# A chunked delta-rule recurrence with a gated MLP behind it: four kinds of small matmuls put into one run, both merges and the keys' products into another, and a first merge that fills all rows

## The chip, the core and the metric

The kernel runs on one core of one Trainium2 chip. The time is device microseconds of one execution. The kernel before takes 634.97 us (median of three executions, 634.14 to 635.45). The execution that was profiled took 633.96 us, of which 631.8 us are the span from the first to the last instruction.

## The reference

Attention by the delta rule, for 4 batches and 8 heads, 768 tokens, head size 48, and then a two-layer MLP with SiLU over all 3072 tokens:

```python
for t in range(S):
    kt, vt, bt = (k_n[:, :, t], v[:, :, t], beta[:, :, t, None])
    y[:, :, t] = np.einsum('bhd,bhde->bhe', q[:, :, t], state)
    v_old = np.einsum('bhde,bhd->bhe', state, kt)
    state = state + bt[:, :, :, None] * np.einsum('bhd,bhe->bhde', kt, vt - v_old)
x = y.transpose(0, 2, 1, 3).reshape(B * S, H * D)          # 3072 x 384
h = x @ w_in                                               # 384 x 2048
out = (h * (1.0 / (1.0 + np.exp(-h)))) @ w_out             # 2048 x 384
```

`k_n` is `k` divided by its norm. Everything is float32.

## The kernel before

The 768 tokens are cut into six chunks (`c` = 0 to 5) of 128, each of two halves of 64 (`hf` = 0, 1). Batches go in two groups (`g` = 0, 1) of two, so that one group has 16 heads; one group's work on one half is 16 matmuls of each kind, each with 48 or 64 rows and columns, and the two groups stand on opposite halves of the 128 rows. For a chunk from 1 on, the recurrence has these steps (`solve`, L1004):

- the triangular system of each head is inverted in blocks of 32, by VectorE, and the blocks of 32 are joined by two rows of products on TensorE, the first and the second merge (`merge`, L793; tile names `py` and `px`, matmuls on L808). The first merge's result is copied to `y`, the second's to `xi`;
- `keys` (L850, matmuls on L854): the state times the keys, added to the values `vf` by VectorE;
- `inner` (L861, L866): the inverse times `vf`, copied by ScalarE to `z`;
- `old` (L928, L932): the queries times the state, into a PSUM bank `pyc`. For the group with `hf != g`, ScalarE then reads a few words of the bank (tile `read`), since `new` adds to the same bank from other rows;
- `update` (L879, L886): keys times `z`, added to the state by VectorE, which the next `keys` and `old` need;
- `new` (L940, L945): scores times `z`, added to the bank of `old`; ScalarE copies the result out (`part`, `xT`).

Beside this stands the MLP of the chunk before: `hidden` (L1081, matmuls on L1088, 128 x 256), and `combine` (L1185, on L1200, 128 x 192), or for chunk 0 `project` (L1120, on L1132). The matmuls of the MLP use the full array of 128 x 128; those of the recurrence use tiles of it, 64 x 64, 64 x 48 or 32 x 32, four at a time.

Each float32 matmul is two passes, and each pass is a weight load and a matmul for the engine, so one matmul of the program is four TensorE instructions (a transpose is two). The trace counts passes.

The order on TensorE is written out by hand. A script of letters (`chunks`, L1656) calls the generators in turn: `s` is one step of the recurrence (`solve`), `r` one step of the MLP (three matmuls of 256 or four of 192), `i` a step of the inversion, `y`, `m`, `k`, `v` preparation and loads. `pin` (L78) binds each engine's instructions into the order in which they are called. So a change of the script moves instructions on all engines at once. In the kernel before, `solve` yields between almost all of the steps above, and the script puts `r` between them: a run of small matmuls, then 4 to 32 big ones, and so on.

## Time and profile before

| What | Value |
|---|---|
| Median of three executions | 634.97 us |
| Profiled execution | 633.96 us |
| its span | 631.8 us |
| TensorE matmuls, weight loads | 9390 passes each, busy 617.7 us and 543.3 us |
| VectorE, ScalarE, GpSimd busy | 415.5, 226.7, 94.0 us |
| Granted TensorE clock, mean | 0.989 |
| DMA queue q8, kind "instruction" | 74 packets, 1.21 MB |

The chain of work that ended last is followed back from the last instruction; a row of it is a start, a length and what ran or was waited for ("issue" is time in which the engine waited for nothing that the profile shows). A timeline row is the start, the length, the engine, line and operation; a matmul's end is modelled, so the distance between the starts says how long something held the engine. A view by windows has the busy time and, in brackets, the count of each engine's instructions. The strips of the DMA view cut a window into 40 equal slices; a digit is the share of the sixteen DMA engines that was busy in it.

### The profile page before, as it was taken

The page shows a single profiled execution, that of the slowest core. Times are in us where ns is not written, and L with a number is a line of the kernel's source. Part 1 is how long each engine was busy: PE and PEld are TensorE (multiplying, and loading weights), DVE is VectorE, ACT ScalarE, POOL GpSimd, SP SyncE. Part 2 cuts the span into 40 slices and gives each one's busy share as a digit, 9 for nine tenths or more (in the row PEclk, how much of TensorE's full clock was granted, in tenths as well). Part 3 has the DMA queues.
Part 4 walks back from the last instruction along what each step waited for, and adds up shares of the span by engine and source line. Part 5 has one row for each costly group of instructions (what it writes and reads, how often), then busy time and mean ns, then how long its engine had stood idle before and what let it go on. Part 6 is the DMA issues. An engine that isn't in the chain of part 4 may idle for free.

```text
span 631.8 us, 21374 instructions
## 1 busy us (share of the span) xinstructions
PE 617.7 (98%) x9390; PEld 543.3 (86%) x9390; DVE 415.5 (66%) x927; ACT 226.7 (36%) x516; POOL 94.0 (15%) x101
## 2 busy tenths in 40 slices
PE   8889989999999999999999999999999999999997
PEld 5578778666799989989989989989989989988997
DVE  6886779999667974546975554976444983345432
ACT  4657873332441122451122451122452122454210
POOL 5234631335020020020020010020002000000000
PEclk9869999999999999999999999999999999999999
DMA  9656506350459360459141359433254024010011
GB/s 175 134 141 199 170 16 149 116 86 4 101 100 186 62 108 4 95 107 188 34 92 20 72 125 156 65 75 44 52 113 95 2 75 62 17 38 1 0 26 26
DMA packets 136941, 52.61 MB, mean 83 GB/s; under 512 B 108672, under 2 KB 130432, under 8 KB 136848
## 3 DMA queue, kind: packets, MB, share of 16 engines
q1 hardware_dynamic: 136512, 51.09, 39.6%
q8 instruction: 74, 1.21, 0.9%
q10 hardware_dynamic: 336, 0.15, 0.1%
q14 instruction: 19, 0.16, 0.1%
HBM read 39.09 MB, written 9.96 MB: 78 GB/s over the span
## 4 chain that ended last, share of the span: by engine, by line
PE 93%; SPq 2%; DMA 1%; issue 1%; ACT 1%; DVE 0%
PE phid L1088 34%; PE px L1200 17%; PE py L1200 13%; PE po L1132 5%; PE pb_c L866 3%; PE pa L539 2%; SPq L144 2%; PE pb_c L1303 2%; PE pb_c L854 2%; PE pyc L945 2%; PE pc L1303 2%; PE pb_c L1132 2%; PE pb_c L886 2%; PE pa L1303 1%; PE pyc L932 1%; PE px L808 1%
## 5 line engine op out<-in xcount | busy, mean ns | idle before, releaser
L1088 PE MATMUL phid<-xT,w_in 128*128 128x256 f32 x960 | 214.9, 382 | 1.9 <-issue 1.7
L1088 PEld LDWEIGHTS phid<-xT,w_in 128*128 128x128 f32 x960 | 180.2, 190 | 26.9 <-issue 2.8
L1098 ACT ACTIVATE gT<-phid 128x512 f32<-128x512 f32 x72 | 42.9, 597 | 115.2 <-PE phid L1088 106.2
L656 DVE SCALAR_TENSOR_TENSOR rank<-g,step,x 128x31 f32<-128x31 f32 (+15 forms) x124 | 49.8, 402 | 23.3 <-DMA g<-blocks 19.8
L1200 PE MATMUL px<-sums_of_w,sums_of_g 128*128 128x192 f32 x320 | 56.6, 329 | 0.0
L1200 PE MATMUL py<-w_out,sums_of_g 128*128 128x192 f32 x320 | 56.2, 328 | 0.0
L1200 PEld LDWEIGHTS px<-sums_of_w,sums_of_g 128*128 128x128 f32 x320 | 52.2, 190 | 0.4
L1200 PEld LDWEIGHTS py<-w_out,sums_of_g 128*128 128x128 f32 x320 | 52.3, 190 | 0.3
L661 DVE TENSOR_TENSOR x<-x,rank 128x31 f32<-128x31 f32 (+15 forms) x124 | 42.5, 342 | 4.3
L477 POOL TENSOR_TENSOR vf<-vf,n_slot 128x768 f32<-128x768 f32 x10 | 14.8, 1492 | 175.4 <-DMA vf<-in_v_dram 129.9
L1183 DVE TENSOR_TENSOR sums_of_g<-gT 128x384 f32<-128x384 f32 (+1 forms) x48 | 24.6, 540 | 14.6 <-ACT gT L1098 14.5
L498 DVE STREAM_TRANSPOSE kq<-stage 128x512 f32<-128x512 f32 x28 | 28.4, 1121 | 6.8 <-DMA stage<-in_q_dram 3.5
L554 ACT COPY xT<-pyc 48x128 f32<-48x128 f32 (+2 forms) x120 | 31.1, 259 | 1.6
L1211 DVE TENSOR_TENSOR o<-o,kept 128x192 f32<-128x192 f32 (+1 forms) x29 | 11.5, 425 | 26.7 <-ACT kept L1208 26.7
L560 POOL COPY g<-x 64x256 f32<-64x256 f32 x4 | 5.0, 1244 | 150.8 <-DVE x L664 150.8
L891 DVE TENSOR_TENSOR state<-state,pb_c 128x384 f32<-128x384 f32 x22 | 11.2, 550 | 24.6 <-PE pb_c L886 24.6
L866 PEld LDWEIGHTS pb_c<-vf,xi 64*64 64x64 f32 x736 | 23.3, 138 | 3.2 <-issue 2.3
L866 PE MATMUL pb_c<-vf,xi 64*64 64x48 f32 x736 | 24.9, 223 | 0.1
L1132 PE MATMUL po<-w_out,gT 128*128 128x384 f32 x64 | 23.7, 491 | 0.0
L1200 PE MATMUL py<-w_out,gT 128*128 128x192 f32 x128 | 23.4, 331 | 0.0
L859 DVE TENSOR_TENSOR vf<-vf,pb_c 128x384 f32<-128x384 f32 x22 | 11.2, 550 | 18.3 <-PE pb_c L854 15.5
L1200 PE MATMUL px<-w_out,gT 128*128 128x192 f32 x128 | 22.4, 327 | 0.0
(293 smaller groups left out, 1094.5 us busy)
## 6 DMA issues: line engine op xcount, KB each, us to landing
vf<-in_v_dram SPq DMA_DIRECT2D x48, 96.0 KB, 2.8
out_dram<-o SPq DMA_DIRECT2D x42, 96.0 KB, 2.2
w_out<-in_moe_w_in_dram SPq DMA_DIRECT2D x4, 768.0 KB, 5.0
sums_of_w<-in_moe_w_out_dram SPq DMA_DIRECT2D x4, 768.0 KB, 4.6
kb<-in_k_dram SPq DMA_DIRECT2D x12, 192.0 KB, 4.5
kb<-in_k_dram SPq DMA_DIRECT2D x24, 96.0 KB, 4.0
raw<-in_moe_w_in_dram SPq DMA_DIRECT2D x3, 768.0 KB, 6.8
blocks<-ap SPq DMA_DIRECT2D x32, 64.0 KB, 1.9
```

Source lines behind the costliest of these rows:

```text
L477: pin(nc.gpsimd.tensor_tensor(out=vf, in0=vf, in1=of, op=ALU.mult))
L498: pin(nc.vector.transpose(out=kqs[c, b][:, :, j, :].rearrange("p a (i m) -> p a m i", i=T), in_=src.rearrange("p a (m d) -> p a m d", d=D) ...
L554: return pin(nc.scalar.copy(to, of))
L656: pin(nc.vector.scalar_tensor_tensor(out=tv, in0=g[:, 0:m, m : m + 1].to_broadcast([P, m, n]), scalar=step[:, m : m + 1], in1=x[:, m : m + ...
L661: yield pin(nc.vector.tensor_tensor(out=x[:, 0:m, m:T], in0=x[:, 0:m, m:T], in1=tv, op=ALU.add))
L866: yield pin(nc.tensor.matmul(pz[rows, n * D : (n + 1) * D], lhsT=xis[g][rows, u * H + 2 * p + e, :], rhs=vfs[c][rows, hf, g * HB + u, p, : ...
L1088: pin(nc.tensor.matmul(ph[:, j * GT : (j + 1) * GT], lhsT=w_in[:, a, (2 * f + j) * P : (2 * f + j + 1) * P], rhs=xTs[c, hf][:, a, :], star ...
L1098: pin(nc.scalar.activation(out=hidden_of(c, hf, f), in_=ph[:], func=ACTF.Silu, scale=-0.5 if in_blocks(c) else 0.5))
L1132: pin(nc.tensor.matmul(pos[i][:, 0:DM], lhsT=hidden_of(0, hf, f // 2)[:, at : at + C], rhs=w_outs[f // HFF][:, f % HFF, :], start=(f == 0) ...
L1183: pin(nc.vector.tensor_tensor(out=sums_of_g[:, k, fs], in0=of[0], in1=of[1], op=op))
L1200: pin(nc.tensor.matmul(to, lhsT=at, rhs=quarter(f, *b) if isinstance(b, tuple) else sums_of_w[b][:, f], start=start and f == 0, stop=f == ...
L1303: pin(nc.tensor.matmul(to[:, i * GT : (i + 1) * GT], lhsT=left(a, slice(f, f + 1))[:, 0], rhs=right(b), start=start and i == 0 and n == 0, ...
```

## The change

Four things change.

1. `made` now issues `inner` and `old` of both groups itself, group `1 - hf` first, and directly behind them `update` and `new`, one group after the other, with the two kinds alternating. Before, `update` of both groups alternated, then `new` of both, and the script stood between `old` and `update`. In the second half of chunk 5 (where nothing needs the state any more) the script still stands before `new`.
2. `merge` as the first merge multiplies by all 64 columns of the weights, so that its products fill all 64 rows of each half; the rows that nobody reads are copied too. One copy of 128 x 512 for each group replaces two of 32 x 512.
3. The script calls three steps together where a chunk begins (`s3`): first merge, `keys`, second merge. This holds for chunks 2 to 5.
4. The counts of `r` around the steps, and the end of the script of chunk 0, are adapted.

```diff
@@ merge
-                    left = aps[c, g][0][even, n // H, n % H, T:W]
-                    to, right = odd, xes[c][even, g * HH + n, :]
+                    left = aps[c, g][0][even, n // H, n % H, :]
+                    to, right = HALVES[k ^ g], xes[c][even, g * HH + n, :]
...
-            for rows in (slice(T, W), slice(W + T, P)):
-                (by_act, by_dve)[g](y[rows, g], of[rows])
+            (by_act, by_dve)[g](y[:, g], of)
@@ update
-        if c == NCH - 1 and hf == 1:
-            return
@@ new
-        copies.append(even_heads(c, g, hf, py))
+        copies.append((g, even_heads(c, g, hf, py)))
+        copies.sort(key=lambda of: of[0])
@@ made
-        together(update(c, 0, hf), update(c, 1, hf))
-        together(new(c, 0, hf), new(c, 1, hf))
-        for copy in copies:
+        gs = (1 - hf, hf)
+        for g in gs:
+            together(inner(c, g, hf), old(c, g, hf))
+        if (c, hf) == (1, 1):
+            follow(c)
+        if (c, hf) == (LAST, 1):
+            yield
+            together(new(c, 0, hf), new(c, 1, hf))
+        else:
+            for g in gs:
+                together(update(c, g, hf), new(c, g, hf))
+        for _, copy in copies:
             next(copy)
@@ solve
-            for g in range(2):
-                together(inner(c, g, hf), old(c, g, hf))
-            if hf == 1:
-                if c == 1:
-                    follow(c)
-            yield
-            made(c, hf)
+            yield from made(c, hf)
@@ chunks
-        5: "r s r2 s r s r2 s r s r s r s r2 s r s r2 s",
+        5: "r2 s3 r2 s r s r s r2 s r s r2 s r3",
```

How the order on TensorE changes where `inner` and `old` of chunk 3's second half end (`pb_c<-vf,xi` is `inner`, `pyc<-kq,state` is `old`, `pb_c<-z,kb` is `update`, `pyc<-ap,z` is `new`). Before:

```order
2349 L866 MATMUL pb_c_74<-vf,xi 64x48
2350 L932 MATMUL pyc<-kq,state_91 64x64
2351 L1200 MATMUL py<-w_out_110,sums_of_g 128x192 x4
2352 L1088 MATMUL phid<-xT,w_in 128x256 x3
2353 L886 MATMUL pb_c_75<-z,kb_77 48x48
2354 L886 MATMUL pb_c_73<-z,kb_77 48x48
```

and after the change:

```order
2350 L865 MATMUL pb_c_74<-vf,xi 64x48
2351 L929 MATMUL pyc<-kq,state_91 64x64
2352 L883 MATMUL pb_c_75<-z,kb_77 48x48
2353 L942 MATMUL pyc<-ap_3805,z 64x64
2354 L883 MATMUL pb_c_75<-z,kb_77 48x48
```

The seven big matmuls between have moved away, `update` follows `old` directly, and alternates with `new` of the same group instead of with `update` of the other.

The same for the end of chunk 3's first merge (`py<-xe,ap`), with `keys` behind it (`pb_c<-state,kq`). Before:

```order
2018 L808 MATMUL py<-xe,ap_3808 32x32
2019 L808 MATMUL py<-xe,ap_3856 32x32
2020 L1200 MATMUL px<-w_out_110,gT 128x192 x4
2021 L1200 MATMUL px<-sums_of_w,gT 128x192 x8
2022 L1200 MATMUL py<-w_out_109,sums_of_g 128x192 x4
2023 L854 MATMUL pb_c_74<-state_90,kq 64x48
```

and after the change:

```order
2024 L808 MATMUL py<-xe,ap_3804 64x32
2025 L808 MATMUL py<-xe,ap_3852 64x32
2026 L853 MATMUL pb_c_74<-state_90,kq 64x48
2027 L853 MATMUL pb_c_75<-state_91,kq 64x48
2028 L853 MATMUL pb_c_74<-state_90,kq 64x48
```

The sixteen big matmuls between have gone, and a product of the first merge is 64 rows high instead of 32; the second merge now follows behind `keys` as it did in this chunk before.

On ScalarE, around chunk 3's merges (`y<-py` and `xi<-px` are the merges' copies, `o<-px` and `o<-py` the MLP's). Before:

```order
227 L1098 ACTIVATE gT<-phid 128x512 x8
228 L554 COPY y<-py 32x512 x2
229 L1227 ACTIVATE o<-px 128x2x192
230 L554 COPY xi<-px 32x16x32 x2
231 L1230 ACTIVATE o<-py 128x192
232 L554 COPY z<-pb_c_73 128x2x4x48
233 L554 COPY z<-pb_c_74 128x2x4x48
234 L554 COPY read<-pyc 128x8
```

and after the change:

```order
228 L1231 ACTIVATE o<-py 128x192
229 L554 COPY y<-py 128x512
230 L554 COPY xi<-px 32x16x32 x2
231 L1234 ACTIVATE o<-px 128x192
232 L554 COPY z<-pb_c_73 128x2x4x48
233 L554 COPY read<-pyc 128x8
234 L554 COPY z<-pb_c_74 128x2x4x48
```

One copy of `y` is left of two, and the read of the bank, which now belongs to the group that comes first, stands between the two copies of `z`.

## The prediction

> **What bounds the kernel now.** First the page: the busy shares, then the shares of the chain that ended last.

> ```profile
> span 631.8 us, 21374 instructions
> ...
> PE 617.7 (98%) x9390; PEld 543.3 (86%) x9390; DVE 415.5 (66%) x927; ACT 226.7 (36%) x516; POOL 94.0 (15%) x101
> ...
> q8 instruction: 74, 1.21, 0.9%
> ...
> PE 93%; SPq 2%; DMA 1%; issue 1%; ACT 1%; DVE 0%
> ```

> TensorE is the bound: 98% busy, 93% of the chain, and nearly nothing waited for. So a gain can only come from the time that TensorE itself takes for its instructions or loses between them. Third, the chain around chunk 4's recurrence, since the change does the same there as in its neighbours.

> ```profile
> 425.53 2.60 PE px L1200 x16
> 428.13 1.22 PE py L808 x82
> 429.35 1.08 PE pb_c L854 x64
> 430.42 2.80 PE px L1200 x16
> ...
> 443.36 0.86 PE pb_c L886 x64
> 444.22 0.36 PE pyc L945 x23
> 444.59 0.23 issue
> 444.82 0.85 PE pyc L945 x41
> 445.67 1.50 PE py L1200 x8
> ...
> 453.64 0.18 PE pb_c L866
> 453.97 0.04 PE pb_c L866 x2
> ...
> 459.75 0.86 PE pb_c L886 x64
> 460.61 0.95 PE pyc L945 x64
> ```

> Three things are to be seen. Sixteen big passes take 2.60 us behind big ones and 2.80 us behind small ones: 0.20 us for a switch. A small run is dense in instructions: `update` and `new` are 128 passes, so 256 instructions with the weight loads, in 0.86 + 0.95 = 1.81 us, or 141 per us; sixteen big passes are 32 instructions in 2.60 us, 12 per us. And inside one `new` stands an "issue" of 0.23 us that waits for nothing: this run lasts 445.67 − 443.36 = 2.31 us, 0.50 more than the 1.81 of its twin at 459.75. Two like it stand elsewhere:

> ```profile
> 252.56 0.42 PE L886 MATMUL pb_c<-z,kb 64*48 64x48 f32 x18 [0.21 <-issue]
> 534.54 0.21 PE L808 MATMUL px<-xi,y 32*32 32x32 f32 x1 [0.24 <-issue]
> ```

> **What the stops are.** Windows between the three places count the instructions (second and third columns: matmuls and weight loads).

> ```profile
> 252.56:444.82 192.26, 192.02 (x2926) 176.90 (x2926) 125.02 (x302) 58.36 (x150) 16.85 (x18) 1.00 0.48 88
> 444.82:534.54 89.72, 89.48 (x1144) 82.00 (x1145) 53.28 (x117) 26.47 (x69) 5.20 (x5) 1.00 0.36 70
> 534.54:576.67 42.13, 42.13 (x742) 37.78 (x743) 20.92 (x40) 20.58 (x50) 0.00 (x0) 1.00 0.09 21
> ```

> 2926 + 2926 = 5852, and with the 36 semaphore waits that the program has there and this view doesn't count, 5888 = 23 x 256. 2289 and 15 make 2304 = 9 x 256. The 1.21 MB in 74 packets of the page are 16 KB each. So the stops stand at a fixed place in a raster of 256 instructions: TensorE reaches the end of what has been loaded. The DMA view shows when the packets go (a window of 6 us in 40 slices from 249 on, then one from 574 on, and the count for 535 to 577):

> ```profile
> DMA  0000004000000000000000000000000400000000
> ```

> ```profile
> DMA  0000000000000000040000000000000000000000
> ```

> ```profile
> q8 instruction: 7, 0.11, 1.2%
> ```

> One packet goes at 249.90, the stop ends at 252.56, and the next goes at 253.65: about 2.55 us from packet to use, 1.15 us from there to the next packet, 3.7 us for a cycle, one at a time. In the quiet stretch behind 534.54 the seventh packet goes at 576.55. By then 1485 + 12 = 1497 instructions have run of the 7 x 256 = 1792 that were there or came: 295 are left, and 307 when the refill was asked for 1.15 us earlier (12 per us). That is the condition: 307 instructions must last 3.7 us. At 12 per us they last 25 us; at 141 per us, 2.2.

> [...]

> **The change, part by part.**

> A. *Joints.* Small runs behind chunk 0 go from 37 to 23 by the order: nine joints between `old` and `update`, five at the merges. Each saves the 0.20 of one switch: 2.8. The first pass of a run of `inner` also stands 0.18 us alone (453.64 above) where two later ones take 0.04; a joined `update` may spare some of this, 0.1 at nine joints. I take −3.7 (−2.8 to −4.2).

> B. *The wider first merge.* Small matmuls of four tiles at a time go by the columns of their weights: 32 in a merge (1.22 us for 128 passes by the rows above, 9.5 ns each), 64 in `new` and `keys` (0.95 and 1.08 for 64: 14.8 and 16.9 ns). A first merge has 128 passes, and its weights go from 32 to 64 columns: by `new` 128 x 5.3 ns = 0.68, by `keys` 0.94; I take 0.8, five times: +4.0 (4.7 at most; 0 if the row count of the stream sets it). The copies:

> ```profile
> 237.73 1.39 DVE L557 COPY y<-py 32x512 f32<-32x512 f32 x2 [0.48 <-PE py L808]
> 260.56 0.48 ACT L554 COPY z<-pb_c 128x384 f32<-128x384 f32 x1 [0.76 <-PE pyc L932]
> 261.50 0.48 ACT L554 COPY z<-pb_c 128x384 f32<-128x384 f32 x1 [0.40 <-PE pb_c L866]
> ```

> Two copies of `y` took 1.39, so one takes 0.70; `keys` with its 1.08 now covers it, 0.3 to spare. If VectorE is in another sum of about that length when the merge ends, up to 0.5 at each of four places is uncovered; I cost it at nothing.

> [...] No row here shows the wider merge itself; those of `new` and `keys` lie on both sides of it.

> C. *`update` and `new` alternating.* Now of one group, with unlike tiles. What alternates today is `inner` with `old`:

> ```profile
> 259.36 0.25 PE L866 MATMUL pb_c<-vf,xi 64*64 64x48 f32 x1
> ...
> 261.38 2.87 PE L1200 MATMUL py<-w_out,sums_of_g 128*128 128x192 f32 x16
> ```

> 2.02 us against 1.81: 0.21 at nine places is 1.9 at most, 0 if order doesn't matter; I take half, +1.0. The waits: the first group's `z` is copied 260.56 to 261.04, before `old` ends; the second's ends at 261.98, when the first group's `update` and `new` (half of 1.81) run until 262.3. So 0.3 of cover; without it up to 0.5 at nine places. ScalarE's reading of the bank goes between the two, and belongs to the group that is done. The transfers aren't issued in these steps other than before, and the MLP's big passes only move: nothing.

> D. *The old stops.* Their places change: −3 x 0.50 = −1.5.

> E. *New stops in the nine joined runs.* 512 instructions in 2.02 + 1.81 = 3.83 us are 134 per us; 307 last 2.3, the refill takes 3.7: a stop of 1.4, and 0.05 to start again as above. Refills are asked for at 449 − 307 = 142 and every 256 from there (449 is where the old stops stand, modulo 256). Counted in the changed order this is 131, 191, 51, 114, 31, 125, 188 and 89 instructions into eight of the runs, whose end is 512: limit and stop fall inside. In chunk 3's first half it is 32 before the run, but there the refill of the merges' run just ahead is still under way, and takes its turn first. All nine stop: 9 x 1.45 = +13.1.

> F. *New stops in the joined merges of chunks 2 to 5.* 256 instructions of the first merge at 256/(1.22 + 0.8) = 127 per us, 128 of `keys` at 119, 258 of the second merge at 210. Chunk 2 asks at 214: its 307 last 0.33 + 1.08 + 0.65 = 2.06, stop 1.64. Chunk 3 at 131: 1.38. Chunk 4 at 32: 1.24, and the next 256 behind that stop last 1.38 of a full cycle: 2.32 more. Chunk 5 at −4: 0.96 and 2.19. Together +9.7.

> Sum: −3.7 + 4.0 + 1.0 − 1.5 + 13.1 + 9.7 = +22.6. The profiled execution took 633.96, so 656.6; the median shown stands 1.0 above that one, so 658. The change trades switches of 0.2 us for stops of 1.4.

> **Rivals.**

> 1. *The loading keeps ahead, and E and F don't come.* For it: most dense runs of today pass without a stop. Place: the thirteen joined runs; price: A to D, −3.7 + 4.0 + 1.0 − 1.5 = −0.2, so 634.8, and 629.6 if the weights' columns and the order cost nothing. It decides as soon as the stops sum to less than 0.2. Against: the raster, and a chunk 0 whose dense work shows more than two cycles' worth:

> ```profile
> 34.80 1.13 issue
> ...
> 38.35 1.14 issue
> ...
> 83.58 1.71 issue
> ```

> Two limits 3.55 us apart, each with a stop, can't be where the loading runs ahead. 0.07, 0.04 of it faster.

> 2. *Fewer stops.* If refills are asked for a little earlier than one reading of the quiet stretch says, or their places are off by some semaphore instructions: with the request anywhere in 256, it lies in the first 203 instructions of a run (so that 307 more still end inside) in 8 of 10 cases, 7 of 9 runs; and a merges' run has only its first stop (1.64 + 1.38 + 1.24 + 0.96 = 5.2). Then 7 x 1.45 + 5.2 = 15.4 for 22.8: 650. For it: only three of 37 runs stop today. Against: those three fit the condition. 0.12.

> 3. *The stops lower the clock.* The last column but two is the granted clock:

> ```profile
> 31.00:46.00 15.00, 12.57 (x561) 11.88 (x560) 12.04 (x24) 7.54 (x16) 4.71 (x3) 0.66 0.50 136
> 46.00:92.00 46.00, 43.69 (x1257) 36.28 (x1253) 33.13 (x71) 36.67 (x72) 23.54 (x17) 1.00 0.47 136
> ```

> Where two stops of 1.1 lie close together it is 0.66, where the one of 1.71 stands, 1.00. Two close ones come in the merges of chunks 4 and 5 alone. If each draws such a stretch, up to 0.34 x 15 = 5.1 apiece, some 8 together: 666. Against: the start of the kernel has other idle time too. 0.13.

> **How the numbers follow.** Forecast 0.68, rivals 0.07, 0.12, 0.13. The cycle read from two slices may be 3.5 to 4.0: fifteen stops by ±0.25 are ±3.8. With A, B and C at their cheap ends (−5.5) or dear ends (+2.5) the likeliest case reaches from 649 to 664. The range takes in rival 2 with a cheap merge (646) and rival 3 (667), and leaves rival 1 out. A change under 0.2% (1.3 us) can't be told from none here. Slower 0.92: all but rival 1 and 0.01 for what I don't see; faster 0.05, the same 0.03.

> **What would show it.** In the changed profile: nine runs of four kinds with an idle "issue" or a gap of about 1.4 us in each, and one or two in each merges' run; all at places that differ by multiples of 256 instructions; instruction packets 3.7 us apart around them; matmuls as many as before; first merges of 2.0 us where no stop lies in them; granted clock 1.00 there. The prediction is wrong if these runs go through in 3.8 us without a gap (rival 1), if gaps stand before `update` and wait for ScalarE's `z` (the cover of 0.3 gone), or if the clock falls after the merges.

## The result and the profile after

The changed kernel takes 667.16 us (median of four executions, 663.82 to 669.80) against 635.03 for the kernel before: a ratio of 1.0505, 95% interval 1.0453 to 1.0558. The forecast was 658, its range ended at 667. The direction, the place and the main mechanism of the loss (TensorE runs out of loaded instructions: fourteen stops of 18.8 us in all, where there were three) are as forecast. The time lies 9 us above it, and a fall of the clock that the forecast had only as a rival came too.

The four executions took 663.82, 665.91, 668.42 and 669.80 us, with mean granted clocks of 0.974, 0.971, 0.964 and 0.964. The profiled one is the slowest, and what follows is an account of it; between the medians the loss is 32.1 us. Its page, as before: span, busy times, and the shares of the chain that ended last.

```profile
span 667.8 us, 21343 instructions
...
PE 635.1 (95%) x9390; PEld 562.4 (84%) x9390; DVE 416.1 (62%) x922; ACT 224.6 (34%) x511; POOL 94.0 (14%) x101
...
PE 91%; issue 4%; DVE 3%; DMA 1%; ACT 0%; SPq 0%; POOL 0%; POOLq 0%; DVEq 0%
```

The passes are as many as before, and the span is 36.0 us longer than 631.8. TensorE is idle for longer, and also busy for 17.4 us longer, with the same passes. The view of waits (engine, line, released by: us in total, times, longest) from 130 to 600 us shows the first part:

```profile
PE pb_c L883 <- issue: 6.6, 4, 2.3
PE pyc L942 <- issue: 5.5, 4, 1.7
PE px L808 <- issue: 4.9, 4, 1.6
PE pb_c L853 <- issue: 1.8, 2, 1.1
```

The three stops of before (252.56, 444.59 and 534.54) have become fourteen, all "issue", none of them a wait for ScalarE, VectorE or a transfer. The chain around chunk 4's joined merges, which answers to the rows from 425 us on of before:

```profile
454.29 2.00 PE py L808 x128
456.28 0.77 PE pb_c L853 x41
457.05 0.76 issue
457.81 0.84 PE pb_c L853 x23
458.65 1.54 PE px L808 x104
460.19 1.26 issue
461.45 0.54 PE px L808 x24
461.99 4.16 PE py L1201 x16
```

The first merge takes 2.00 us instead of 1.22. The run stops twice, as counted ahead. And the sixteen big passes behind it take 4.16 us, not 2.80: passes like these and the wider first merges are most of the busy part of the loss. The windows of low granted clock behind chunk 0 (third column from the right), four of six; chunk 3's merges (6.83 us from 355.50) and chunk 1's second half (3.41 us from 174.60) have the others:

```profile
253.10:259.93 6.83, 6.78 (x90) 6.28 (x93) 2.82 (x5) 1.48 (x3) 0.00 (x0) 0.50 0.01 2
...
457.90:464.73 6.83, 5.57 (x160) 5.28 (x161) 3.62 (x7) 1.15 (x2) 0.00 (x0) 0.50 0.02 5
485.21:488.62 3.41, 3.41 (x9) 2.66 (x8) 0.92 (x1) 1.32 (x6) 0.00 (x0) 0.50 0.86 133
560.30:570.54 10.24, 9.18 (x197) 8.46 (x201) 3.84 (x7) 1.48 (x3) 0.00 (x0) 0.50 0.02 3
```

At or behind each joined run of merges stand 6.8 to 10.2 us of half clock, and behind two of the nine other runs 3.4 us. Before there was none of this behind chunk 0.

That the stops are those of the raster is seen in the counts between them (matmuls and weight loads are the second and third columns):

```profile
457.81:461.45 3.64, 2.38 (x127) 2.15 (x127) 1.02 (x2) 0.00 (x0) 0.00 (x0) 0.51 0.02 5
461.45:470.99 9.54, 7.94 (x255) 7.51 (x256) 3.29 (x6) 2.51 (x6) 0.00 (x0) 0.83 0.02 3
```

254 are two short of 256, and 255 + 256 = 511 are one short of 512. From each of the fourteen stops to the next the counts fall short of a multiple of 256 by 1 to 15 and never go over it; semaphore waits, which this view leaves out, would fill the rest. The instruction queue q8 carries one packet of 16 KB for each 256: 45 from the end of the first stop to the end of the last (156.28 to 574.68). The kernel before shows the same: 23 packets for the 23 x 256 between its first two stops, 9 for the 9 x 256 to the third. And one of the nine runs, in chunk 3's first half, has no stop:

```profile
362.68:366.51 3.83, 3.83 (x257) 3.77 (x256) 0.55 (x1) 1.02 (x3) 0.00 (x0) 1.00 0.02 4
```

It is the measure for the other eight. The account of the 36.0 us, from the lengths of the runs and of the big passes behind them in the two traces (the two values at full clock in the fourth row are from the trace of the narrow merge, below):

| Part | us |
|---|---|
| nine runs of four kinds: 48.98 in all, less 9 x 3.84 | +14.4 |
| four merges' runs: 28.25 in all, less 4 x (2.00 + 1.08 + 1.22) | +11.1 |
| 16 big passes behind each of these: 5.42, 5.13, 4.16, 5.42 instead of 2.80 | +8.9 |
| big passes behind two other runs: 11.54 and 9.80, at full clock 9.86 and 8.11 | +3.4 |
| first merge, 5 x (2.00 - 1.22) | +3.9 |
| fourteen joints by 0.20 | -2.8 |
| the three old stops | -1.4 |
| chunk 0 (its big passes start at 90.74 instead of 91.89) | -1.2 |
| sum | +36.3 |

### The profile page after: what moved, and what is told of

It is laid out like the page before. It is cut to its first block, busy times and chain, and to the rows that moved or that the text cites. A ratio compares the mean times of both kernels' runs of the same rounds, so it can differ in the third digit from the quotient of the medians.

```text
span 667.8 us, 21343 instructions
## 1 busy us (share of the span) xinstructions
PE 635.1 (95%) x9390; PEld 562.4 (84%) x9390; DVE 416.1 (62%) x922; ACT 224.6 (34%) x511; POOL 94.0 (14%) x101
## 3 DMA queue, kind: packets, MB, share of 16 engines
q8 instruction: 74, 1.21, 0.8%
## 4 chain that ended last, share of the span: by engine, by line
PE 91%; issue 4%; DVE 3%; DMA 1%; ACT 0%; SPq 0%; POOL 0%; POOLq 0%; DVEq 0%
PE phid L1089 32%; PE px L1201 16%; PE py L1201 13%; PE po L1133 5%; PE pb_c L865 3%; PE pa L539 2%; PE pyc L942 2%; PE pb_c L853 2%; PE pb_c L1304 2%; PE pc L1304 2%; PE pb_c L1133 2%; PE py L808 1%; PE px L808 1%; PE pa L1304 1%; PE pb_c L883 1%
## 5 line engine op out<-in xcount | busy, mean ns | idle before, releaser
L1089 PE MATMUL phid<-xT,w_in 128*128 128x256 f32 x960 | 217.4, 385 | 1.0 <-issue 0.9
L1089 PEld LDWEIGHTS phid<-xT,w_in 128*128 128x128 f32 x960 | 182.8, 192 | 27.4 <-issue 1.9
L656 DVE SCALAR_TENSOR_TENSOR rank<-g,step,x 128x31 f32<-128x31 f32 (+15 forms) x124 | 49.8, 401 | 20.4 <-DMA g<-blocks 16.9
L1201 PE MATMUL px<-sums_of_w,sums_of_g 128*128 128x192 f32 x320 | 61.0, 344 | 0.0
L1201 PE MATMUL py<-w_out,sums_of_g 128*128 128x192 f32 x320 | 57.6, 333 | 0.0
L1201 PEld LDWEIGHTS px<-sums_of_w,sums_of_g 128*128 128x128 f32 x320 | 55.9, 201 | 0.5
L1184 DVE TENSOR_TENSOR sums_of_g<-gT 128x384 f32<-128x384 f32 (+1 forms) x48 | 26.5, 568 | 24.0 <-ACT gT L1099 15.2
L554 ACT COPY xT<-pyc 48x128 f32<-48x128 f32 (+2 forms) x120 | 31.1, 259 | 1.6
L942 PE MATMUL pyc<-ap,z 64*64 64x64 f32 x704 | 22.2, 221 | 5.5 <-issue 5.5
L942 PEld LDWEIGHTS pyc<-ap,z 64*64 64x64 f32 x704 | 20.0, 134 | 8.1 <-issue 8.1
L1201 PE MATMUL py<-w_out,gT 128*128 128x192 f32 x128 | 26.7, 365 | 0.0
L883 PE MATMUL pb_c<-z,kb 64*48 64x48 f32 x704 | 20.3, 208 | 6.6 <-issue 6.6
```

The source lines that it names most:

```text
L554: return pin(nc.scalar.copy(to, of))
L656: pin(nc.vector.scalar_tensor_tensor(out=tv, in0=g[:, 0:m, m : m + 1].to_broadcast([P, m, n]), scalar=step[:, m : m + 1], in1=x[:, m : m + ...
L883: yield pin(nc.tensor.matmul(pu[of, n * D : (n + 1) * D], lhsT=kbufs[c % 2][rows, g * HB + u, p, e, 0:D], rhs=zbuf[rows, g * HB + u, hf, p ...
L942: yield pin(nc.tensor.matmul(py[HALVES[1 - e], C * p + W * u : C * p + W * (u + 1)], lhsT=zbuf[rows, g * HB + u, hf, p, :], rhs=aps[c, g][ ...
L1089: pin(nc.tensor.matmul(ph[:, j * GT : (j + 1) * GT], lhsT=w_in[:, a, (2 * f + j) * P : (2 * f + j + 1) * P], rhs=xTs[c, hf][:, a, :], star ...
L1201: pin(nc.tensor.matmul(to, lhsT=at, rhs=quarter(f, *b) if isinstance(b, tuple) else sums_of_w[b][:, f], start=start and f == 0, stop=f == ...
```

## The experiments

The kernels of the first four experiments ran together, beside executions of the kernel before with a median of 633.49 us; the next four beside 634.47; the last two beside 633.21. What is compared are the ratios to these; since the expectations name times beside the 635.03 us from above, each ratio is also given as a time beside that. Lines of the script are shown as far as they change, without their ends. The theory: TensorE reaches the end of what is loaded in the joined runs, and where such a stop meets a run of small tiles, the clock falls as well. Rivals: the stops are waits for a result (the copies of `z`, a PSUM bank); the steps themselves got dearer; the clock falls whenever these steps stand together.

**The runs of four kinds apart again.** `made` yields behind `old` in chunks 2 to 5, and the script puts a step there:

```diff
@@ made
+        if c > 1:
+            yield
...
-            yield
@@ chunks
-        3: "r6 s3 r2 s r s r s r2 s v r2 s
+        3: "r6 s3 r s r s r s r s r s r s v r2 s
```

> The changed kernel, but in chunks 2 to 5 one or two steps of the MLP stand between old and update again; merges and keys stay joined. Theory (TensorE reaches the end of what is loaded, and then the clock falls): of the seven joined runs there, six lasted 5.14 to 5.90 us against 3.84 for the seventh, which has no stop, 10.4 us over; that goes, some 1 us in short stops stays, seven switches of 0.2 to 0.3 come back, and the low clock behind chunk 5's recurrence (1.6 us) goes: 667.2 - 10.4 - 1.6 + 1.0 + 1.8 = 658 (655 to 660), and no stop over 0.7 us in these runs. Rival (the merges' run and the low clock behind it cost nearly all): not under 663.

Measured: 660.97 us, ratio 1.0431 (1.0389 to 1.0472) against 1.0505, or 662.4 us beside 635.03. The stops in these runs, L883 and L942 in the waits, fell from 6.6 + 5.5 to 2.3 + 0.9, of which 2.3 and 0.9 are chunk 1's two runs, which were left joined:

```profile
PE px L808 <- issue: 5.4, 4, 1.7
PE pb_c L883 <- issue: 2.3, 1, 2.3
...
PE pyc L942 <- issue: 0.9, 1, 0.9
```

The time came 4 us short of the expected gain. It lies between the theory (655 to 660) and the rival (not under 663), with an interval of 659.7 to 665.0 that reaches both, so the time alone doesn't decide; that the stops went is what speaks for the theory. Behind the merges there is now only one step of the MLP before `inner`, so `inner` and `old` fall into the low clock too: they took 2.73, 2.29, 2.65 (a stop of 0.37 in it) and 3.10 us in the four chunks instead of 2.02.

**The merges apart again.** In chunks 2 to 5 the script's `s3` becomes `s r s r s`, with the steps taken from ahead of it (in chunk 5, one of the two from the end):

```diff
-        3: "r6 s3 r2 s
+        3: "r4 s r s r s r2 s
```

> The changed kernel, but the two merges and the keys' products of chunks 2 to 5 have a step of the MLP between them again; the nine other runs stay joined. Theory: the four runs of 642 instructions lost 11.1 us in stops and the big passes behind them 8.9 us to the low clock; both go, some 1.5 us of stops stays, and eight switches of 0.2 come back: 667.2 - 11.1 - 8.9 + 1.5 + 1.6 = 650 (647 to 653), with a granted clock of 1.00 in the 16 big passes of 192 behind the merges, 2.8 us instead of 4.2 to 5.4. Rival (the clock falls because of the joined inner, old, update and new ahead or behind): the clock stays low there, and not under 656.

Measured: 655.87 us, 1.0350 (1.0310 to 1.0390), or 657.3 beside 635.03. By the time alone this is where the rival stands (not under 656), and not the theory (647 to 653); what the two differ in, the clock behind the merges, is seen in the trace. The big passes behind the second merge are at full clock again, 2.80 us:

```profile
453.24:456.04 2.80, 2.80 (x27) 2.58 (x17) 2.58 (x5) 1.15 (x2) 0.00 (x0) 1.00 0.03 6
```

So the low clock there was the merges' runs' own, not that of the nine others, and the rival falls. But 7 us of the expected gain are missing. Between the two profiled executions the span fell by 13.5 us (667.8 to 654.3): 9.4 us of stops in the merges' runs, 8.9 of low clock behind them and 1.7 behind chunk 1's recurrence are gone; against that stand 1.6 for eight switches, 1.2 in chunk 0, and 1.5 that the nine other runs are longer (50.43 instead of 48.98). This makes 15.7, and some 2 us are left open. The longer runs are seen in the chain: in chunk 4's first half one stop has become two.

```profile
450.93 1.02 PE px L808 x70
451.94 0.98 issue
...
457.54 1.10 issue
460.64 1.73 issue
```

That run went from 5.69 to 7.12 us, and chunk 3's, which had none, got one (3.84 to 5.17). It may be that a stop in the merges had given the loading time for the next, and that without it the next limits are reached early. This isn't shown: each step that was moved also shifts the places of the raster by 16 instructions, and the two weren't tried apart.

**A narrow first merge.** `merge` as it was before, in the changed script:

```diff
@@ merge
-                    left = aps[c, g][0][even, n // H, n % H, :]
-                    to, right = HALVES[k ^ g], xes[c][even, g * HH + n, :]
+                    left = aps[c, g][0][even, n // H, n % H, T:W]
+                    to, right = odd, xes[c][even, g * HH + n, :]
...
-            (by_act, by_dve)[g](y[:, g], of)
+            for rows in (slice(T, W), slice(W + T, P)):
+                (by_act, by_dve)[g](y[rows, g], of[rows])
```

> The changed kernel with the first merge's products 32 rows high as before, and its copies split again. The first merge of chunk 1 goes from 2.00 to 1.22 us. If nothing hides it, five times 0.78: 663.3. Theory: in the joined merges' runs TensorE then only reaches the end of what is loaded earlier, and the stop gets longer by what the merge got shorter in those where the refill was asked for before or in the first merge (chunks 3, 4 and 5): some 2 us of 3.9 come back, 665 (662 to 667).

Measured: 663.85 us, 1.0477 (1.0444 to 1.0509). The five runs with a first merge became 0.78, 0.76, 0.39, -0.33 and 0.74 us shorter, 2.3 of the 3.9. Beside 635.03 the ratio is 665.3 us, with an interval of 663.2 to 667.3: it is at the theory's 665, but takes in the 663.3 of a merge that nothing hides, so it doesn't decide between them. A line of its waits shows what the one wide copy of `y` was good for:

```profile
PE px L808 <- DVE y L557: 0.9, 2, 0.5
```

With two copies per group the second merge waits for `y` twice, once `keys` alone stands between; with one copy it never did.

**The raster moved.** 32 more products ahead of chunk 1, the same as the one that stands there:

```diff
-                pin(nc.tensor.matmul(unread[:, 0:T], lhsT=ident[:], rhs=pick[:], start=True, stop=True))
+                for _ in range(33):
+                    pin(nc.tensor.matmul(unread[:, 0:T], lhsT=ident[:], rhs=pick[:], start=True, stop=True))
```

> The changed kernel with 32 more products (128 instructions) on TensorE ahead of chunk 1, each the same as one that is there; nothing else differs. Theory: the stops stay at instructions 449 + 256 j, so they move to other work: the merges' run of chunk 2 and of chunk 3 has two stops instead of one, that of chunk 4 one instead of two, and the nine runs of four kinds stop at other passes. The sum of stops stays about as now (23 to 25 us); with 3 to 5 us for the added products 668 to 673. Rival (the stops are waits for a result, the z copies or a bank): they stay at the same passes of the same runs.

Measured: 677.23 us, 1.0689 (1.0650 to 1.0729), or 678.8 beside 635.03. Chunk 3's merges' run, with one stop in the changed kernel, has two, and chunk 4's, with two, has one:

```profile
360.48 2.00 PE py L808 x128
363.06 0.74 issue
...
366.01 1.63 issue
...
468.09 2.00 PE py L808 x128
470.09 1.08 PE pb_c L853 x64
471.63 1.25 issue
```

Chunk 2's second half, which stopped for 2.0 us, took 3.84 us with no stop. In chunk 2 the second stop came just behind the run, in the first big passes, instead of in it. The stops follow the count of instructions, not the work: the rival of a wait for a result falls. The time is higher than expected mainly at the added thin products: the 66 passes that stand there took 10.8 us (from 87.58), where 3 to 5 were allowed for, and the granted clock was one half from 91.33 on:

```profile
91.33:104.98 13.65, 13.65 (x139) 12.74 (x139) 5.27 (x15) 0.00 (x0) 0.14 (x1) 0.50 0.28 101
```

**The two inner changes alone.** The script and the yields of the kernel before, with the wide first merge (and its one copy) and the alternation of `update` and `new` (and the order of the groups that goes with it):

```diff
@@ merge (against the kernel before)
-                    left = aps[c, g][0][even, n // H, n % H, T:W]
-                    to, right = odd, xes[c][even, g * HH + n, :]
+                    left = aps[c, g][0][even, n // H, n % H, :]
+                    to, right = HALVES[k ^ g], xes[c][even, g * HH + n, :]
...
@@ made
-        together(update(c, 0, hf), update(c, 1, hf))
-        together(new(c, 0, hf), new(c, 1, hf))
...
+            for g in gs:
+                together(update(c, g, hf), new(c, g, hf))
```

> The kernel before (its script, every run as short as there) with the two changes inside the steps alone: the first merge fills all rows, and update and new alternate, one group behind the other. No joined runs, so none of the new stops and no low clock behind the merges. Theory: five merges by 0.78 = 3.9 and nothing for the alternation (the one joined run without a stop took 3.84 us, as 2.02 + 1.81 before): ratio 1.006 (1.004 to 1.008). By the term C of the prediction, 1.0 us more: 1.008. Rival (the steps themselves carry a wait for z that the joined runs hid among their stops): over 1.010.

Measured: 638.11 us beside 634.47, 1.0048 (1.0021 to 1.0075), 3.0 us. There is no stop and no wait behind 130 us in its profile. But the alternation isn't free here: `update` and `new` take 1.98 us in chunk 3's first half (from 349.46 in the chain) where they took 1.81 before (from 347.80), which is 1.5 us for nine. With 3.9 for the five merges, less 1.4 for the three old stops and 0.9 because chunk 1's first merge starts that much earlier, this makes 3.1 (the profiled spans differ by 3.3). So the expectation's "nothing for the alternation" is wrong, and its time came out by luck, since it had left out the old stops as well. In the joined run the 0.17 isn't seen: 2.02 + 1.98 would be 4.00, and the run without a stop takes 3.84. The other 4.5% of the loss are the joining, with the clock.

**One step between `keys` and the second merge.** `s3` becomes `s2 r s`:

```diff
-        4: "r6 s3 r2 s
+        4: "r5 s2 r s r2 s
```

> The changed kernel with one step of the MLP (16 big passes' worth of instructions, 1.3 to 1.5 us) between keys and second merge of chunks 2 to 5; first merge and keys stay joined. Theory: where a refill was asked for in the first merge it still is late once per run (chunks 4 and 5, about 1.3 us each, and 0.9 behind it), chunk 2 has none and chunk 3 none: 4 to 5 us of stops left of 11.1, and the clock falls less often, since a window of 3.41 us that ends here holds big passes: 667.2 - 6.5 - 4 to 9 + 0.8 = 652 to 658. Rival (the clock falls whenever merge and keys stand together): as merges_apart in stops, but 8.9 us of low clock stay, 660 or more.

Measured: 658.59 us, 1.0390 (1.0345 to 1.0435), or 659.8 beside 635.03, above the expected 652 to 658 and just under the rival's 660; again the trace decides. This is the clearest look at the clock, since the same pair of steps comes with and without a stop. Chunk 2 and chunk 4:

```profile
245.24 2.00 PE py L808 x128
247.24 1.08 PE pb_c L853 x64
248.32 1.50 PE px L1201 x8
...
445.08 2.00 PE py L808 x128
447.07 0.88 PE pb_c L853 x49
447.96 1.65 issue
449.61 0.67 PE pb_c L853 x13
450.28 2.86 PE px L1201 x8
```

3.08 us of small tiles without a stop leave the clock up, and the eight big passes take 1.50 us. With a stop of 1.65 in them they take 2.86, and the clock is one half for 10.24 us:

```profile
448.11:458.35 10.24, 8.74 (x162) 8.15 (x163) 3.75 (x7) 1.48 (x3) 0.00 (x0) 0.50 0.01 3
```

Chunk 3 went as chunk 2, and chunk 5 as chunk 4, with 3.41 us of half clock (550.51 to 553.92). So it isn't the joining of `merge` and `keys` as such.

**The loads of queries later.** The order of the calls alone:

```diff
@@ made
-        if (c, hf) == (1, 1):
-            follow(c)
@@ solve
-                if c > 1:
-                    follow(c)
                 yield
             yield from made(c, hf)
+            if hf == 1:
+                follow(c)
```

> The changed kernel, but the loads of the next chunk's queries are issued behind the second half's joined run of a chunk instead of ahead of or inside it. Theory (a refill shares the DMA engines with these loads, which are 90% busy where stops are long): the stops of chunk 1's, 2's and 4's second half, 2.57, 2.01 and 1.94 us, come down to 1.3 to 1.6 us, by some 2 us in all. The time isn't the point: what waits for these loads comes later by several us, so 665 to 680. Rival (those stops are long for another reason): they stay at 1.9 and above.

Measured: one execution, 688.47 us. The strips of the DMA view show the busy share of the engines from 167.5 to 175 us, around the stop in chunk 1's second half. The changed kernel, and then the stop in its chain:

```profile
DMA  0000000006369999999999999996210000000003
```

```profile
171.32 2.35 issue
```

With the later loads, strip and stop:

```profile
DMA  0000000000000000000000400000000000000000
```

```profile
172.99 1.27 issue
```

The gaps between passes at the three places went from 2.57, 2.01 and 1.94 us to 1.49, 1.45 and 1.46. So these stops are 0.5 to 1.1 us shorter without the loads beside them. For the first of the three this is clear: in four other kernels here that leave the loads where they were (the first three and the one with a step between `keys` and the second merge) it lasts 1.82 to 2.35 us. For the second it isn't: three of these have 1.23 to 1.54 there. The whole time is of no use here: the next chunk's transposes wait for the late loads (12.5 us in its waits).

**A better version, tried three times.** First, the kernel before with steps of the MLP moved ahead of `update` in chunks 0, 2 and 4, and to between `keys` and the second merge in chunk 5 (the line from the script of chunk 0 is a part from its middle):

```diff
-        2: "s r4 s2 r2 s r s r s2 r d r s r v r2 s r2 s y
+        2: "s r4 s2 r2 s r2 s r s2 d r s r v r2 s r2 s y
...
-p l s l4 p l2 s r l f l4 f l f l2 p l s l2 s f r f r l r l2 p g
+p l s l4 p l2 s r2 l f l4 f l f l2 p l s l2 s f r f l r l2 p g
```

> The kernel before with nothing but five steps of the MLP moved to places ahead of update, where TensorE ran to the end of what was loaded: one in each of chunks 2, 4 and 5, and in chunk 0 one step from behind new to ahead of update. Theory: the stops of 0.4 to 0.5 at chunks 2, 4 and 5 go (1.3 us), and 1.2 of the 1.7 behind chunk 0's new: ratio 0.996 (0.995 to 0.998). Rival (the stops only move to other passes): 1.000.

Measured: 637.37 us beside 634.47, 1.0046 (1.0023 to 1.0069): half a per cent slower. The stop of 1.7 us in chunk 0 went, but the step had covered a transfer and a copy, for which TensorE now waits (waits from 84 to 140 us):

```profile
PE phid L1088 <- DMA xT<-part: 1.9, 1, 1.9
PE pa L539 <- ACT xT L554: 1.2, 1, 1.2
```

Second, the same for chunks 2, 4 and 5 alone, with the loads kept in place:

```diff
-        4: "s2 r4 s r2 s r s r2 s r s r2 s r3 s2 d v
+        4: "s2 r4 s r2 s r2 s r s r s r2 s r3 s2 d v
...
-        5: "r s r2 s r s r2 s r s r s r s r2 s r s r2 s",
+        5: "s r2 s r2 s r2 s r s r s r s r2 s r s r2 s",
```

> The kernel before with one step of the MLP moved to ahead of update in chunks 2 and 4, and to between keys and second merge in chunk 5; chunk 0 and the place of the loads as before. Theory: the three stops of 0.4 to 0.5 us go, and one of 0.3 to 0.4 may come elsewhere (the moved step is 16 instructions): 0.9 us less, ratio 0.9986 (0.997 to 1.000), which this measurement can hardly tell from 1. Rival (a moved step uncovers something, as it did in chunk 0): 1.002 or more.

Measured: 633.05 us beside 633.21, 0.9997 (0.9976 to 1.0017). No change: its trace has three stops of 0.3 to 0.4 us at other places of the raster.

Third, the kernel before with dummy products in chunk 0's long run of small tiles:

```diff
@@ joins(0, ...), at three of its ten places
-        lambda: (),
+        lambda: (busy(3, wide=192),),
```

> The kernel before with three times three big products (128 x 192, 1 us each time) that nobody needs, put into the run of 560 small passes of chunk 0, where the granted clock is one half for 10 us and two refills come late by 1.1 us each. Theory: the big passes give the refills time and keep the clock up; 2.3 us of stops and some 3 us of half clock go, 3 us are paid: 2.3 us less there, ratio 0.996, if the 36 added instructions move no late stop to the later runs (by their raster two or three of 0.4 to 1.3 us come): 0.997 to 1.001. Rival (the clock stays low): 1.003 to 1.006.

Measured: 641.92 us, 1.0142 (1.0114 to 1.0169). This is more than the rival's 1.003 to 1.006. The clock stayed low all the same, 13.65 us instead of 10.24:

```profile
37.59:51.24 13.65, 13.50 (x292) 11.89 (x296) 8.45 (x16) 5.63 (x11) 3.17 (x2) 0.50 0.55 118
```

And late stops came elsewhere, one of 0.89 us in chunk 3 and one of 1.70 in chunk 4, the latter right behind the first merge and `keys`; behind it the clock is one half for another 3.4 us:

```profile
438.83 1.70 issue
440.53 4.18 PE px L1200 x15
```

What else makes up the loss is open. No version that beats the kernel before was found.

## Why the prediction was right or wrong

- *What the stops are, and where.* Right. Of the fifteen that were counted, fourteen came; the one in chunk 3's first half didn't, where the refill was asked for 32 instructions ahead of the run. Both stops of chunk 4's and of chunk 5's merges came, and none elsewhere behind chunk 0. Rivals 1 and 2 are out.
- *A, the joints.* The account closes to 0.3 us with 0.20 each, the lower end, -2.8 instead of -3.7. This is a net of A and C, though: by the run with the two inner changes alone, the nine joined `update` and `new` spare 0.16 us each, more than the 0.1 that was put down for it, and the alternation eats that up.
- *B, the first merge.* 2.00 us instead of 1.22, 3.9 for five, where 4.0 was said: a pass with 64 columns of weights took 15.6 ns, one with 32 9.5. One copy of `y` is covered by `keys`, as said.
- *C, the alternation.* In the account nothing is left for it, since the run without a stop takes 3.84 us, as 2.02 + 1.81 before. By itself it costs 0.17 us a run, 1.5 in all, rather more than the 1.0 that was said. `z` is never waited for.
- *D.* As said, -1.4.
- *E, the nine runs.* 14.4 instead of 13.1. One stop less, but three of the eight of 1.9 to 2.6 us instead of 1.45. A step that failed is the one value of 3.7 us for a refill, taken from stretches in which the DMA engines carried nothing else. These three stand beside loads of queries, and the run with later loads brings them down to 1.5, though only the longest of them clearly because of the loads.
- *F, the merges.* 11.1 instead of 9.7; part of it is the second merge itself at half clock (128 passes in 1.54 + 0.54 instead of 1.22 in chunk 4).
- *The clock.* This is the step that put the time out of the range: "Against: the start of the kernel has other idle time too", by which the fall of the clock became a rival of 0.13 that adds 8 us, and "Two close ones come in the merges of chunks 4 and 5 alone". It came behind all four merges' runs, and behind two of the nine: 12.3 us of longer big passes. Two close stops aren't needed: chunk 2's and chunk 3's merges had a single one, of 1.58 and 0.94 us. The forecast and this rival together (666) come close to the 667.16, but partly by luck: the account is of an execution that took 2.6 us more than the median, and in it the clock cost 12.3 us, not 8.
- *Small slips that move nothing.* 1.15 us at 12 instructions per us are 14, so the 307 should be 309; and the low end of rival 1 is 634.97 - 3.7 - 1.5 = 629.8, not 629.6.

The six stretches of half clock behind chunk 0 in the changed kernel last 3.41, 6.83 or 10.24 us, one, two or three times 3.41; with the raster moved, and with the dummy products in chunk 0, one of 13.65 us comes, four times that. The pair of steps left the clock at 1.00 in 3.08 us of small tiles without a stop, and at 0.50 from 448.11 on where a stop of 1.65 us (from 447.96) stood in them. What decides it wasn't measured by itself. That big passes inside such a stretch keep the clock up, as the expectation for the pair of steps has it, no run shows.

What stays open: some 2 us between the account and the gain in the profiled spans with the merges apart, and whether the small tiles or the stop in them brought the half clock. Neither the stop nor the length of the run decides alone: six of the eight runs of four kinds with a stop (0.93 to 1.80 us in it, 5.14 to 5.91 us long) left the clock at 1.00, while `merge` and `keys` of 4.42 us with a stop of 1.14, in chunk 5 of the run with a step behind `keys`, halved it. Why these differ isn't shown.

## What to carry to other kernels

Count instructions, not only time: here small fp32 matmuls eat 120 to 210 instructions a microsecond (128 of `keys` in 1.08 us, 256 of the second merge in 1.22), and twelve of the thirteen joined runs of 512 or 640 of them outran the loading although their operands were there. The big matmuls between small ones, which look like a cost of 0.2 us each, give the loading its time: put back into seven runs of four kinds they took the stops at `update` and `new` from 12.1 us to 3.2, all of it in the two runs left joined, and put back between the merges they left the clock behind those of chunks 4 and 5 at 1.00. A table of where the instruction counter stands at each run (here 449 + 256 j, by the count of the program's order) told beforehand which of them stop, with one miss in fifteen, and a stop that is removed can come back in the next run.
